# Scores of last queries and early blocks, made for an even and an odd head pair together

## The chip, the cores and the metric

The kernel runs on one core of a Trainium2 chip. The metric is the device time of one execution, in microseconds (us). The core has TensorE (PE in the profile; its weight loads are PEld), VectorE (DVE), ScalarE (ACT), GpSimd (POOL) and SyncE (SP, which issues the DMAs). SBUF is the working memory, PSUM the eight banks into which TensorE writes.

## What is computed

Attention of 4 batches x 8 heads over 576 positions with heads 64 wide, with a mask by blocks of 64 (a query sees its own block and all before it), then two MLPs over the 2304 tokens, 512 wide.

```python
scores = scale * np.matmul(q, k.transpose(0, 1, 3, 2))
mask = block_i >= block_j            # blocks of 64
scores = np.where(mask, scores, -1000000000.0)
attn = softmax(scores)               # exp(s - max) / (sum + 1e-09)
x = np.matmul(attn, v)               # -> (2304, 512)
x = (sigmoid(x @ w_gate) * (x @ w_val)) @ w_out      # d_ff 1536
h = x @ w_in                                          # d_ff 2048
return np.maximum(0.01 * h, h) @ w_out2
```

## The kernel before

**Stages.** Tokens are worked on in stages. Batch 0's attention runs alone at the front. Stage 0 is the MLP over tokens 0 to 767, with batch 1's attention beside it; stage 1 is the MLP over tokens 768 to 1279, with the attention of batches 2 and 3 beside it; a last stage does the other 1024 tokens with no attention (`pair_unit`, its products at L1149). The MLP's products beside attention are made in units of twelve matmuls at L1301, each into one of three PSUM banks (`b_mm`), which VectorE or ScalarE drains. Since 768 is not a multiple of 576, stage 0 also needs the first 192 queries of batch 1 and stage 1 the first 128 of batch 2 ahead of time: these are the early blocks (`first_blocks`, L688).

**Order.** Nothing is issued as it is written. Each step is an `op` with an engine, a cost, what it reads, writes and uses, and a due time; `Plan.order` (L149) simulates the five engines with these costs and fixes the order of instructions on each. A ring of buffers is handed out in the order in which the program asked for it. An engine then follows its order and waits on semaphores, so anything behind a waiting instruction on its engine waits too. A changed cost or dependency moves everything that the plan places after it.

**A head pair.** `attention` (L407) takes four pairs of heads (a = 0, 1) of a batch in turn. Queries and keys of a pair lie in one tile `tqk`, head 0 on partitions 0 to 63 and head 1 on 64 to 127; there are 3 such tiles, and 2 for V. `made_scores` (L599) makes the scores of query tiles 0 and 1, and of 2 and 3; `softmax` (L466) has VectorE mask, scale and find the least (L485), ScalarE take the exponential (L500), VectorE invert the sum (L510, L513) and ScalarE or GpSimd multiply (L518, L520); `transposed` (L622) turns the probabilities with TensorE (L633) into `tp` banks, of which there are two, and VectorE or ScalarE copies them to `p_t`; `p_v` (L648) is the product with V (L657). A batch whose first queries are made early starts with query tile 1.

**Last queries.** 576 is four tiles of 128 and a rest of 64. For the rest both heads share one tile of scores: `of_last` (L545) puts head a on output partitions 64a to 64a + 63, from input partitions 64a to 64a + 63, so that the two products use the upper left and the lower right quarter of TensorE's array (64 rows, 64 columns; the profile writes 64\*64). Beside the MLP the first 512 keys go to a `tp` bank and the last 64 to the free end of a score bank, at the line that also makes all other scores (L428); `alone`, they are two pieces of 288. `later` holds products that are issued with the next group of scores: the last queries' scores, then last P·V (L584, `last_p_v`) and P·V. The transposed probabilities (L569) of the last queries go to a tile of their own, `p_l` (named `last`), whose lower half is zero for the last 64 keys.

**Early blocks.** `first_blocks` makes the scores of all its pairs at L730, each pair's head 0 in the upper left and head 1 in the lower right quarter, in two groups of blocks by width, each with one score bank and one op. Batch 1 has two calls of two pairs (blocks of 64, 128 and 192 keys) at the end of batch 0's attention, batch 2 one call of four pairs (64 and 128 keys) ahead of batch 1's fourth pair (L1421). P·V of early blocks is at L773.

In the code a float32 product is one call; in the trace it stands as two matmul records of the same shape.

Of the kernel before, what the change touches and what calls it, by code (L numbers as in the profile page):

```python
# [18 lines left out]
P = 128  # L19
# [205 lines left out]
def block_attention_then_two_mlps(  # L225
# [51 lines left out]
    p_l = const.tile([P, NKT * P], F32, name="last")  # L277
# [23 lines left out]
    for c, n, turns_of in ((0, P, 2), (1, 2 * P, 2), (2, 3 * P, 1), (3, 4 * P, 1), (NKT - 1, S, 1)):  # L301
        for a in range(1 if n == S else 2):
            for k in range(turns_of):
                pp[c, a, k] = Lazy(lambda x=at_col, n=n: both[:, x:x + n])
                at_col += n
    assert at_col <= 16 * TN
    for k, x in (("first", (3, 0, 0)), ("second", (3, 1, 0))):
        pp[k] = pp[x]
    r_acc = ring("acc", 1, [P, 4 * SL])
# [97 lines left out]
    def attention(b, start, length, alone, others=()):  # L407
# [13 lines left out]
        def of_scores(products, toks, tqk):  # L421
# [3 lines left out]
            def f():  # L425
                for ps, col, row, a, q0, nq, k0, nk in products:
                    half = slice(a * D, a * D + D)
                    nc.tensor.matmul(  # L428
                        ps[row:row + nq, col:col + nk], lhsT=tqk[half, 0, q0:q0 + nq], rhs=tqk[half, 1, k0:k0 + nk],
                        start=True, stop=True,  # L430
                    )

            used = list(dict.fromkeys(x[0] for x in products))
            return sum(0.82e-3 * x[7] for x in products), f, [(tqk, 0), (tqk, 1)], toks, [tqk, *used]

        def scores(products, tqk, t, slack=slack):
            stretch([of_scores(products, list(dict.fromkeys(x[0] for x in products)), tqk)], t, slack)


        later = []  # L440
# [25 lines left out]
        def softmax(tiles, places, masked, t):  # L466
# [5 lines left out]
            for i, pieces in enumerate(tiles):  # L472
                x = places[i]
                p_tok, claim, keep = ("pp", *x), [], []
                if x[0] in pp:
                    w = pieces[0][2]
                    pt = Lazy(lambda x=x, w=w: pp[x[0]][:, x[1] - places[0][1]:x[1] - places[0][1] + w])
# [49 lines left out]
        def pair(i):  # L527
# [17 lines left out]
            def of_last(pieces):  # L545
# [9 lines left out]
            def last_queries(t):  # L555

                if alone:
                    pieces = [(p, 0, S // 2, p) for p in (bank(), bank())]
                    scores(of_last(pieces), tqk, t)
                else:  # L560
                    pieces = beside
                ((pt, p_tok),) = softmax([pieces], [(NKT - 1, 0, 0)], False, t)
                for part, (j0, j1) in enumerate(((0, NKT - 1), (NKT - 1, NKT))):
# [3 lines left out]
                    def f(tp=tp, nr=nr, j0=j0, j1=j1):  # L567
# [5 lines left out]
                    copy(  # L573
                        n, lambda nr=nr, j0=j0, n=n: p_l[:nr, j0 * P:j0 * P + n], lambda tp=tp, nr=nr, n=n: tp[:nr, :n],
                        [tp], [("last", part)], [tp], t + 4.4, True,
                    )

                def last_p_v(t):
                    px = (b_mm if alone else b_tp).tile()

                    def f():
                        for j in range(NKT):
                            for a in range(2):
                                nc.tensor.matmul(  # L584
                                    px[a * D:a * D + D, :BLK], lhsT=tv[:, a, j],
                                    rhs=p_l[:, j * P + a * BLK:j * P + (a + 1) * BLK], start=j == 0, stop=j == NKT - 1,
# [3 lines left out]
                        NKT * 0.116, f, [(tv, 0), (tv, 1), ("last", 0), ("last", 1)], [px], [px, tv],  # L590
                        lambda: split(S - BLK, S, "D", t + 0.8, px, [px]),
# [7 lines left out]
            def made_scores(cs, t):  # L599
# [905 lines left out]
```

## Time and profile before

| | |
|---|---|
| median of 3 runs | 985.93 us (985.16 to 987.45) |
| profiled execution | 985.49 us, its span 983.7 |
| granted TensorE clock | 1.0 of full speed |
| busy share of the span | PE 98%, DVE 79%, ACT 56%, POOL 17% |
| bytes moved | 227.52 MB, mean 231 GB/s |

The span runs from the first to the last instruction of the program; what lies around it belongs to the time too. PE's share counts the modelled ends of pipelined matmuls, so one that is always busy can still have started its matmuls later than possible: the start of the next operation is the safer measure of what a group takes. A wait is listed with what ended it. Rows of the timeline give the start, the length over all merged records, the engine, the line, the tile written and read, the array shape (rows\*columns), the tile of data, and how many records (x).

### The profile page before, as it was taken

What the parts mean: (1) busy time and instruction counts of PE and PEld (TensorE: products, weight loads), DVE (VectorE), ACT (ScalarE), POOL (GpSimd) and SP (SyncE); (2) the same over time, 40 slices, a digit from 0 to 9 for tenths busy, and PEclk for the clock granted to TensorE, in tenths of its full rate; (3) what the DMA queues carried; (4) which work ended last, traced back from release to release, by engine and by line L of the source; (5) the groups of instructions that cost most, each with busy time, mean ns of one, the idle gap of its engine ahead of it and who ended that gap; (6) DMA issues with size and microseconds to landing.
All of it is one profiled execution on the core that took longest, in us unless ns stands there. A gap on an engine that the chain in (4) does not pass through costs nothing.

```text
span 983.7 us, 15675 instructions
## 1 busy us (share of the span) xinstructions
PE 968.5 (98%) x5468; PEld 780.4 (79%) x5468; DVE 777.4 (79%) x1658; ACT 549.6 (56%) x1103; POOL 163.1 (17%) x172
## 2 busy tenths in 40 slices
PE   7999999999999999999999999999999999999998
PEld 4688888879888888778777877778888877888886
DVE  6989989889989847778789988985538479958656
ACT  7988776576766516455655575444526134744521
POOL 2422001221102101213432232120002021100000
PEclk9999999999999999999999999999999999999999
DMA  7488886856875636989888887877565555665664
GB/s 212 139 288 268 265 288 218 265 186 227 277 266 188 214 121 232 311 278 296 302 283 282 290 262 252 294 255 249 179 204 194 189 183 160 200 212 182 198 195 147
DMA packets 92718, 227.52 MB, mean 231 GB/s; under 512 B 9952, under 2 KB 29920, under 8 KB 92640
## 3 DMA queue, kind: packets, MB, share of 16 engines
q1 hardware_dynamic: 92640, 226.53, 69.6%
q8 instruction: 43, 0.70, 0.3%
q14 instruction: 35, 0.29, 0.1%
HBM read 150.47 MB, written 76.02 MB: 230 GB/s over the span
## 4 chain that ended last, share of the span: by engine, by line
PE 94%; DVE 2%; ACT 2%; DMA 1%; issue 0%; SPq 0%; ACTq 0%; DVEq 0%
PE mm L1301 47%; PE sc L1149 18%; PE tp L1149 9%; PE mm L1149 4%; PE tp L633 3%; PE sc L428 3%; PE pa L657 2%; PE tp L428 2%; PE tp L569 1%; DMA w<-ds 1%; PE mm L657 1%; PE tp L584 1%; ACT both L500 1%; ACT both L518 1%; DVE x L1221 0%; DMA qk<-in_qk 0%
## 5 line engine op out<-in xcount | busy, mean ns | idle before, releaser
L1301 PE MATMUL mm<-x,w 128*128 128x512 f32 (+2 forms) x1008 | 234.2, 384 | 0.0
L1301 PEld LDWEIGHTS mm<-x,w 128*128 128x128 f32 x1008 | 179.9, 188 | 38.5 <-issue 5.2
L1301 PE MATMUL mm<-g,w 128*128 128x512 f32 (+1 forms) x792 | 163.7, 358 | 0.0
L1301 PEld LDWEIGHTS mm<-g,w 128*128 128x128 f32 x792 | 130.2, 189 | 23.0 <-issue 2.4
L1149 PE MATMUL sc<-both,w 128*128 128x512 f32 x480 | 128.2, 390 | 0.1
L1149 PEld LDWEIGHTS sc<-both,w 128*128 128x128 f32 x480 | 89.9, 188 | 19.9 <-ACT wf L342 0.5
L500 ACT ACTIVATE both<-both,nm 128x256 f32<-128x256 f32 (+5 forms) x148 | 84.1, 570 | 28.3 <-DVE nm L485 27.6
L901 POOL TENSOR_TENSOR wf<-mag,rnd 128x512 int32<-128x512 int32 x28 | 37.3, 1332 | 205.9 <-DVE w L355 107.2
L887 ACT ACTIVATE mag<-raw 128x512 f32<-128x512 f32 x68 | 45.6, 671 | 42.8 <-POOL wf L901 18.1
L1301 PE MATMUL mm<-xa,w 128*128 128x256 f32 x480 | 63.6, 285 | 0.0
L1301 PEld LDWEIGHTS mm<-xa,w 128*128 128x128 f32 x480 | 60.8, 191 | 3.3 <-issue 0.8
L355 DVE TENSOR_TENSOR g<-gf,g 128x512 fp32r<-128x512 f32 (+2 forms) x73 | 56.8, 779 | 3.0 <-ACT g L342 3.0
L520 POOL TENSOR_SCALAR both<-both,r 128x256 f32<-128x256 f32 (+6 forms) x54 | 34.9, 653 | 114.3 <-DVE r L513 95.7
L342 ACT ACTIVATE g<-gf 128x512 fp32r<-128x512 f32 (+2 forms) x61 | 40.0, 657 | 24.1 <-DVE gf L1332 12.7
L518 ACT ACTIVATE both<-both,r 128x384 f32<-128x384 f32 (+6 forms) x94 | 48.7, 567 | 7.1 <-DVE r L513 7.0
L485 DVE CUSTOM_DVE_ANT_0 both<-sc,mask 128x256 f32<-128x256 f32 (+6 forms) x101 | 39.4, 423 | 16.1 <-PE sc L428 16.1
L1362 DVE TENSOR_TENSOR acc<-mm,acc 128x512 f32<-128x512 f32 (+1 forms) x60 | 35.8, 598 | 18.8 <-PE mm L1301 18.6
L1221 DVE TENSOR_TENSOR x<-sc,x 128x512 f32<-128x512 f32 x44 | 30.1, 689 | 22.3 <-PE sc L1149 22.2
L895 DVE SCALAR_TENSOR_TENSOR mag<-raw,mag 128x512 int32<-128x512 int32 x68 | 47.4, 698 | 0.3
L1301 PE MATMUL mm<-sg,w 128*128 128x512 f32 (+1 forms) x216 | 47.2, 354 | 0.0
L428 PE MATMUL sc<-qk 64*128 64x384 f32 (+5 forms) x228 | 41.9, 415 | 5.1 <-DMA qk<-in_qk 5.1
L355 DVE TENSOR_TENSOR w<-wf,w 128x512 fp32r<-128x512 f32 x68 | 46.5, 684 | 0.2
(255 smaller groups left out, 1843.7 us busy)
## 6 DMA issues: line engine op xcount, KB each, us to landing
w<-wd SPq DMA_DIRECT2D x102, 512.0 KB, 4.6
raw<-in_w SPq DMA_DIRECT2D x68, 512.0 KB, 4.4
wd<-w SPq DMA_DIRECT2D x68, 512.0 KB, 4.1
ds<-raw SPq DMA_DIRECT2D x68, 512.0 KB, 5.2
w<-ds SPq DMA_DIRECT2D x68, 512.0 KB, 4.3
qk<-in_qk SPq DMA_DIRECT2D x32, 288.0 KB, 5.7
w<-wd SPq DMA_DIRECT2D x68, 128.0 KB, 3.8
v<-in_v SPq DMA_DIRECT2D x32, 160.0 KB, 3.5
```

The costliest lines, as they stand in the source:

```text
L342: nc.scalar.activation(dst(), src(), AF.Copy)
L355: engines[e].tensor_tensor(dst(), a(), f32(b()), ALU.subtract)
L428: nc.tensor.matmul(ps[row:row + nq, col:col + nk], lhsT=tqk[half, 0, q0:q0 + nq], rhs=tqk[half, 1, k0:k0 + nk], start=True, stop=True,)
L485: nc.vector.tensor_tensor_reduce(out=pt[:, n:n + width], in0=ps[:, col:col + width], in1=mask[:, 4 * P + BLK - width:] if masked else mask ...
L500: nc.scalar.activation(pt[:, :n], pt[:, :n], AF.Exp, bias=nm[:, k - 1:k], scale=-1.0, accum_out=sm[:, i:i + 1],)
L518: nc.scalar.activation(pt[:, :n], pt[:, :n], AF.Copy, scale=r[:, i:i + 1])
L887: op("act", c_act(n), lambda: nc.scalar.activation(mag[:], words(1).bitcast(F32), AF.Abs), [raw], [mag], [raw, mag], d - 8)
L895: op("dve", c_dve(n), lambda: nc.vector.scalar_tensor_tensor(out=mag[:].bitcast(I32), in0=words(1).bitcast(I32), scalar=-0x40000000, in1=m ...
L901: engines[e].tensor_tensor(wf[:].bitcast(I32), mag[:].bitcast(I32), rnd[:], ALU.add)
L1149: nc.tensor.matmul(p[:, :n], lhsT=wt[:, wl, at * P:(at + 1) * P], rhs=view[:, xl], start=first and k == 0 and wl + xl == 0, stop=k == 1 an ...
L1301: nc.tensor.matmul(ps[:, :n], lhsT=ws[:, wl, k * P:(k + 1) * P], rhs=srcs[k]()[:, xl, hs], start=k == 0 and wl + xl == 0, stop=k == 3 and ...
L1362: op("dve", c_dve(n), lambda: nc.vector.tensor_tensor(a(), ps[:, :n], a(), ALU.add), [ps], toks_a, [ps, *host], e)
```

## The change

Beside the MLP, an even pair no longer makes the scores of its last queries. It leaves them to the odd pair that follows: `of_last` takes a `turn`, and in an odd pair (turn 1) head a's product goes to the other output half, so its two heads use the upper right and lower left quarter. The odd pair then issues one op with both pairs' products, alternating between the pairs, into two `tp` banks for the 512 keys and two score banks for the 64; its cost to the plan is halved. Softmax, transpositions and last P·V of the even pair are made right before those of the odd one; both last P·V come with the scores of the pair after that. `first_blocks` takes one score bank for its even and one for its odd pairs, turned in the same way, and makes all scores in one op; batch 2's call moves ahead of batch 1's third pair. The tile `p_l` goes: transposed probabilities of last queries lie in places of `p_t` that the causal order leaves free, one set for each turn, and two ops on GpSimd write the zeros. The probabilities of query tiles 0 and 1 have one set of places instead of two, those of last queries two instead of one. Nothing else is computed, and no product is dropped or added.

```diff
@@ -274,7 +274,6 @@
-    p_l = const.tile([P, NKT * P], F32, name="last")
@@ -298,14 +297,25 @@
-    for c, n, turns_of in ((0, P, 2), (1, 2 * P, 2), (2, 3 * P, 1), (3, 4 * P, 1), (NKT - 1, S, 1)):
-        for a in range(1 if n == S else 2):
-            for k in range(turns_of):
-                pp[c, a, k] = Lazy(lambda x=at_col, n=n: both[:, x:x + n])
-                at_col += n
+    for c, n in ((0, P), (1, 2 * P), (2, 3 * P), (3, 4 * P), (NKT - 1, S)):
+        for a in range(2):
+            pp[c, a] = Lazy(lambda x=at_col, n=n: both[:, x:x + n])
+            at_col += n
     assert at_col <= 16 * TN
-    for k, x in (("first", (3, 0, 0)), ("second", (3, 1, 0))):
+    for k, x in (("first", (3, 0)), ("second", (3, 1))):
         pp[k] = pp[x]
+
+    def p_last(turn, j):
+
+        if j < NKT - 1:
+            return p_t[:, 3 - turn, j // 2, j % 2 * P:(j % 2 + 1) * P]
+        return p_t[:, 1, 0, :P] if turn else p_t[:, 3, 0, 2 * P:3 * P]
+
+    for turn in range(2):
+        op(
+            "pool", 0.3, lambda turn=turn: nc.gpsimd.memset(p_last(turn, NKT - 1)[BLK:], 0.0), (), [("zeros", turn)], [both],
+            0.0,
+        )
...
@@ -418,26 +428,27 @@
-        def of_scores(products, toks, tqk):
+        def of_scores(products, toks, share=1.0):
...
-                for ps, col, row, a, q0, nq, k0, nk in products:
+                for tqk, ps, col, row, a, q0, nq, k0, nk in products:
...
-            used = list(dict.fromkeys(x[0] for x in products))
-            return sum(0.82e-3 * x[7] for x in products), f, [(tqk, 0), (tqk, 1)], toks, [tqk, *used]
-
-        def scores(products, tqk, t, slack=slack):
+            qks, used = [list(dict.fromkeys(x[k] for x in products)) for k in range(2)]
+            cost = share * sum(0.82e-3 * x[8] for x in products)
+            return cost, f, [(x, a) for x in qks for a in range(2)], toks, [*qks, *used]
+
+        def scores(products, t, slack=slack):
+            stretch([of_scores(products, list(dict.fromkeys(x[1] for x in products)))], t, slack)
+
+
+        later, waits = [], []
...
@@ -542,24 +553,24 @@
+            turn = 0 if alone else i % 2
+
+            def of_last(pieces, turn=turn, tqk=tqk):
                 n, r = 0, []
                 for p, col, width, _ in pieces:
-                    r += [(p, col, a * BLK, a, S - BLK, BLK, n, width) for a in range(2)]
+                    r.append([(tqk, p, col, (a ^ turn) * BLK, a, S - BLK, BLK, n, width) for a in range(2)])
                     n += width
                 return r
...
-            def last_queries(t):
+            def last_queries(t, lasts, pieces=None):
 
                 if alone:
                     pieces = [(p, 0, S // 2, p) for p in (bank(), bank())]
-                    scores(of_last(pieces), tqk, t)
-                else:
-                    pieces = beside
-                ((pt, p_tok),) = softmax([pieces], [(NKT - 1, 0, 0)], False, t)
+                    scores([y for x in of_last(pieces) for y in x], t)
+                ((pt, p_tok),) = softmax([pieces], [(NKT - 1, turn)], False, t)
...
-                    copy(
-                        n, lambda nr=nr, j0=j0, n=n: p_l[:nr, j0 * P:j0 * P + n], lambda tp=tp, nr=nr, n=n: tp[:nr, :n],
-                        [tp], [("last", part)], [tp], t + 4.4, True,
-                    )
+                    if part:
+                        to, of = (lambda: p_last(turn, NKT - 1)[:BLK]), (lambda tp=tp, n=n: tp[:BLK, :n])
+                    else:
+                        to = lambda: p_t[:, 3 - turn, :, :2 * P]
+                        of = lambda tp=tp, n=n: tp[:, :n].rearrange("p (a q) -> p a q", a=2)
+                    copy(n, to, of, [tp], [("last", turn, part)], [tp, both], t + 4.4, True)
...
+                                half = a ^ turn
                                 nc.tensor.matmul(
                                     px[a * D:a * D + D, :BLK], lhsT=tv[:, a, j],
-                                    rhs=p_l[:, j * P + a * BLK:j * P + (a + 1) * BLK], start=j == 0, stop=j == NKT - 1,
+                                    rhs=p_last(turn, j)[:, half * BLK:(half + 1) * BLK], start=j == 0, stop=j == NKT - 1,
...
-                        NKT * 0.116, f, [(tv, 0), (tv, 1), ("last", 0), ("last", 1)], [px], [px, tv],
-                        lambda: split(S - BLK, S, "D", t + 0.8, px, [px]),
+                        NKT * 0.116, f, [(tv, 0), (tv, 1), ("last", turn, 0), ("last", turn, 1), ("zeros", turn)], [px],
+                        [px, tv, both], lambda: split(S - BLK, S, "D", t + 0.8, px, [px]),
...
-                if cs[0] < 2 and not alone:
-                    p = b_tp.tile()
-                    beside.extend([(p, 0, 4 * P, p), (ps[cs[0], 0], 3 * P, BLK, (ps[cs[0], 0], "beside"))])
-                    later.insert(0, lambda t: of_scores(of_last(beside), [x[3] for x in beside], tqk))
+                if cs[0] < 2 and turn:
+                    for k in range(2):
+                        p = b_tp.tile()
+                        beside.append([(p, 0, 4 * P, p), (ps[cs[0], k], 3 * P, BLK, (ps[cs[0], k], "beside"))])
+                    products = [of_last(beside[0], *waits[0][1:]), of_last(beside[1])]
+                    later.insert(0, lambda t: of_scores(
+                        [z for x in zip(*products) for y in x for z in y], [x[3] for xs in beside for x in xs], 0.5
+                    ))
                 scores(
-                    [(ps[c, a], cols[c], 0, a, c * P, P, 0, (c + 1) * P) for c in cs for a in range(2)], tqk, t,
+                    [(tqk, ps[c, a], cols[c], 0, a, c * P, P, 0, (c + 1) * P) for c in cs for a in range(2)], t,
...
-                done = softmax([[made[x]] for x in xs], [(c, a, i % 2 if c < 2 else 0) for c, a in xs], True, t)
+                done = softmax([[made[x]] for x in xs], xs, True, t)
...
-                last_queries(at[NKT - 1])
...
-                last_queries(t)
+                if turn:
+                    waits.pop()[0](t, lasts, beside[0])
+                    last_queries(t, lasts, beside[1])
+                else:
+                    waits.append((last_queries, turn, tqk))
...
-            groups, at = [[]], 0
-            for k, width in enumerate(widths):
-                if at + m * width > 512:
-                    groups.append([])
-                    at = 0
-                groups[-1].append((k, at))
-                at += m * width
+            ps = [b_sc.tile(), b_sc.tile()]
+            tiles, at = [[], []], [0, 0]
+            for i in range(m):
+                for k, width in enumerate(widths):
+                    tiles[i % 2].append((k, i, at[i % 2], width))
+                    at[i % 2] += width
+
+            def f():
+                x = x_qk()
+                for xs in zip(*tiles):
+                    for p, (k, i, col, width) in zip(ps, xs):
+                        for a in range(2):
+                            half, row = slice(a * D, a * D + D), (a ^ i % 2) * BLK
+                            nc.tensor.matmul(
+                                p[row:row + BLK, col:col + width], lhsT=x[half, i, 0, k * BLK:(k + 1) * BLK],
+                                rhs=x[half, i, 1, :width], start=True, stop=True,
+                            )
+
+            stretch([(
+                sum(0.82e-3 * x[3] for xs in tiles for x in xs), f, [(tqk, i, a) for i in range(m) for a in range(2)], ps,
+                [tqk, *ps],
+            )], t)
...
-            for (place, tok), ks in zip((("first", ("pp", 3, 0, 0)), ("second", ("pp", 3, 1, 0))), groups):
...
-                def f(p=p, tiles=tiles):
-                    x = x_qk()
-                    for k, i, col, width in tiles:
-                        for a in range(2):
-                            half = slice(a * D, a * D + D)
-                            nc.tensor.matmul(
-                                p[half, col:col + width], lhsT=x[half, i, 0, k * BLK:(k + 1) * BLK], rhs=x[half, i, 1, :width],
-                                start=True, stop=True,
-                            )
-
-                stretch([(
-                    sum(0.82e-3 * 2 * x[3] for x in tiles), f, [(tqk, i, a) for i in range(m) for a in range(2)], [p], [tqk, p],
-                )], t)
-                done = softmax([[(p, col, width, p)] for _, _, col, width in tiles], [(place, x[2], tok) for x in tiles], False, t)
-                for x, y in zip(tiles, done):
+            for (place, tok), p, xs in zip((("first", ("pp", 3, 0)), ("second", ("pp", 3, 1))), ps, tiles):
+                done = softmax([[(p, col, width, p)] for _, _, col, width in xs], [(place, x[2], tok) for x in xs], False, t)
+                for x, y in zip(xs, done):
                     soft[x[0], x[1]] = *y, tok
...
+                                row = 3 * P + (a ^ i % 2) * BLK
-                                    rhs=p_t[:nr, jj, aa, 3 * P + a * BLK:3 * P + (a + 1) * BLK],
-                                    start=j == 0, stop=j == js[-1],
+                                    rhs=p_t[:nr, jj, aa, row:row + BLK], start=j == 0, stop=j == js[-1],
...
-                attention(1, starts[0] + 3, length - SPREAD, False, [(2, (0, 1, 2, 3), 3)])
+                attention(1, starts[0] + 3, length - SPREAD, False, [(2, (0, 1, 2, 3), 2)])
...
-        nc.gpsimd.memset(p_l[BLK:, (NKT - 1) * P:], 0.0)
```

## Rows read from the trace of the kernel before

**Rows 1.** The page, part 1: busy time, share of the span and instructions per engine.

```profile
PE 968.5 (98%) x5468; PEld 780.4 (79%) x5468; DVE 777.4 (79%) x1658; ACT 549.6 (56%) x1103; POOL 163.1 (17%) x172
```

**Rows 2.** Busy time by stretch: window, length, engines' busy us, granted clock, DMA share, GB/s.

```profile
300.00:340.00 40.00, 40.00 (x238) 34.31 (x237) 37.25 (x73) 25.15 (x48) 6.61 (x6) 1.00 0.60 204
```

**Rows 3.** The page, part 4: the chain that ended last, by engine.

```profile
PE 94%; DVE 2%; ACT 2%; DMA 1%; issue 0%; SPq 0%; ACTq 0%; DVEq 0%
```

**Rows 4.** PE's waits: what waited for what, us in total, times, longest.

```profile
PE sc L428 <- DMA qk<-in_qk: 5.1, 2, 4.8
PE tp L1149 <- DMA w<-ds: 2.1, 2, 1.6
PE tp L1149 <- DVE x L355: 0.9, 1, 0.9
...
PE sc L1149 <- DVE x L1221: 0.8, 1, 0.8
```

**Rows 5.** Timeline of PE, 206 to 209 us: the last queries of one pair.

```profile
206.94 1.08 PE L428 MATMUL tp<-qk 64*64 64x512 f32 x4
207.85 0.28 PE L428 MATMUL sc<-qk 64*64 64x64 f32 x4
208.06 0.80 PE L584 MATMUL tp<-last,v 128*64 128x64 f32 x20
```

**Rows 6.** The same timeline cut to 206.9 to 207.0 us.

```profile
206.94 0.65 PE L428 MATMUL tp<-qk 64*64 64x512 f32 x2
```

**Rows 7.** Timeline of PE, 70.72 to 70.78 us: early blocks' P·V, then last queries.

```profile
70.60 0.27 PE L773 MATMUL pa<-both,v 64*64 64x64 f32 x2
70.62 0.64 PE L428 MATMUL tp<-qk 64*64 64x512 f32 x1
70.70 0.22 PE L773 MATMUL pa<-both,v 64*64 64x64 f32 x2
```

**Rows 8.** Timeline of PE, 293.74 to 293.80 and 302.0 to 302.2 us.

```profile
293.75 0.27 PE L773 MATMUL tp<-both,v 64*64 64x64 f32 x2
...
302.09 0.60 PE L428 MATMUL tp<-qk 64*128 64x512 f32 x2
```

**Rows 9.** Timeline of PE, early blocks of batch 1 (45) and batch 2 (248).

```profile
45.58 1.54 PE L730 MATMUL sc<-qk 64*64 64x64 f32 x24
47.05 0.87 PE L657 MATMUL mm<-both,v 128*64 128x256 f32 x8
...
248.60 0.68 PE L730 MATMUL sc<-qk 64*64 64x64 f32 x16
249.21 0.80 PE L584 MATMUL tp<-last,v 128*64 128x64 f32 x20
...
251.89 1.09 PE L730 MATMUL sc<-qk 64*64 64x128 f32 x16
252.91 0.97 PE L1301 MATMUL mm<-x,w 128*128 128x512 f32 x3
```

**Rows 10.** Timeline of DVE, 438 to 440 us: a pair's last queries.

```profile
438.90 0.69 DVE L485 CUSTOM_DVE_ANT_0 both<-tp,mask 128x512 f32<-128x512 f32 x1
...
439.65 0.28 DVE L485 CUSTOM_DVE_ANT_0 both<-sc,mask,nm 128x64 f32<-128x64 f32 x1
```

**Rows 11.** The chain in order of time, 600 to 620 us: one MLP unit.

```profile
608.72 2.74 PE mm L1301 x12
```

**Rows 12.** Timeline of PE, 23.3 to 24.2 us, batch 0's attention.

```profile
23.34 0.87 PE L633 MATMUL tp<-ident,both 128*128 128x128 f32 x6
24.14 0.37 PE L428 MATMUL sc<-qk 64*128 64x128 f32 x1
```

**Rows 13.** Timeline of PE, 360 to 375 us: end of batch 1's attention.

```profile
360.11 0.80 PE L584 MATMUL tp<-last,v 128*64 128x64 f32 x20
...
368.81 1.59 PE L1301 MATMUL mm<-xa,w 128*128 128x256 f32 x12
```

**Rows 14.** The page, part 6: DMA issues of V, KB each, us to landing.

```profile
v<-in_v SPq DMA_DIRECT2D x32, 160.0 KB, 3.5
```

More of the change, by code (lines that the diff above doesn't have):

```diff
@@ L431, in f @@
                     )
-            used = list(dict.fromkeys(x[0] for x in products))
-            return sum(0.82e-3 * x[7] for x in products), f, [(tqk, 0), (tqk, 1)], toks, [tqk, *used]
-        def scores(products, tqk, t, slack=slack):
-            stretch([of_scores(products, list(dict.fromkeys(x[0] for x in products)), tqk)], t, slack)
-        later = []
+            qks, used = [list(dict.fromkeys(x[k] for x in products)) for k in range(2)]
[4 more added lines that the diff above has]
+        later, waits = [], []
         def stretch(parts, t, slack=slack):
@@ L476, in softmax @@
                     w = pieces[0][2]
-                    pt = Lazy(lambda x=x, w=w: pp[x[0]][:, x[1] - places[0][1]:x[1] - places[0][1] + w])
+                    pt = Lazy(lambda x=x, w=w: pp[x[0]][:, x[1]:x[1] + w])
                     claim, keep = ([], [x[2]]) if i else ([x[2]], [])
@@ L543, in split @@
                 keep(b, i, n0, n1, parts, t, p, base, reads)
-            def of_last(pieces):
+            turn = 0 if alone else i % 2
+            def of_last(pieces, turn=turn, tqk=tqk):
                 n, r = 0, []
                 for p, col, width, _ in pieces:
-                    r += [(p, col, a * BLK, a, S - BLK, BLK, n, width) for a in range(2)]
+                    r.append([(tqk, p, col, (a ^ turn) * BLK, a, S - BLK, BLK, n, width) for a in range(2)])
                     n += width
@@ L676, in pair @@
                     query_tiles(cs, made_scores(cs, at[cs[0]]), at[cs[0]])
-                last_queries(at[NKT - 1])
+                last_queries(at[NKT - 1], lasts)
             else:
@@ L712, in first_blocks @@
             widths = [(k + 1) * BLK for k in range(nb)]
-            groups, at = [[]], 0
-            for k, width in enumerate(widths):
-                if at + m * width > 512:
-                    groups.append([])
-                    at = 0
-                groups[-1].append((k, at))
-                at += m * width
-            soft = {}
-            for (place, tok), ks in zip((("first", ("pp", 3, 0, 0)), ("second", ("pp", 3, 1, 0))), groups):
-                p = b_sc.tile()
-                tiles = [(k, i, at + i * widths[k], widths[k]) for k, at in ks for i in range(m)]
-                def f(p=p, tiles=tiles):
-                    x = x_qk()
-                    for k, i, col, width in tiles:
-                        for a in range(2):
-                            half = slice(a * D, a * D + D)
-                            nc.tensor.matmul(
-                                p[half, col:col + width], lhsT=x[half, i, 0, k * BLK:(k + 1) * BLK], rhs=x[half, i, 1, :width],
-                                start=True, stop=True,
-                            )
-                stretch([(
-                    sum(0.82e-3 * 2 * x[3] for x in tiles), f, [(tqk, i, a) for i in range(m) for a in range(2)], [p], [tqk, p],
-                )], t)
-                done = softmax([[(p, col, width, p)] for _, _, col, width in tiles], [(place, x[2], tok) for x in tiles], False, t)
-                for x, y in zip(tiles, done):
```

## The prediction

> **What bounds the kernel now.** I read the page first: TensorE (PE) is busy for 98% of the span [rows 1], and in the stretch where VectorE is fullest its granted clock is 1.00, the 2.4 GHz level [rows 2]. The chain that ended last is PE for 94% [rows 3]. PE's list of waits shows what is left: 5.1 us for the first load at the start, and then single waits of up to 1.6 us, the largest in the last stage (L1149) [rows 4]. While attention runs beside the MLP PE has no gap to speak of: 40.00 busy in 40 us [rows 2]. So a microsecond of PE work taken out anywhere after the start should come off the end, as long as no other engine gets in its way; the sum is a sum of PE time. It is made against the profiled execution, 985.49 us (span 983.7 and 1.8 around it); the median of the runs is 985.93, 0.44 above.
>
> **Part 1, the last queries.** In one pair the scores of queries 512 to 575 are two pieces, 512 and 64 keys wide, for two heads. From the start of the first to the start of what follows they take 208.06 - 206.94 = 1.12 us: 0.91 for the 512 columns, 0.21 for the 64 [rows 5]. Each product stands as two records (four for two products [rows 5]), so 0.91 is two steps of some 0.43 us and a switch of 0.05. Both heads already share these steps: two records stand within 0.65 us [rows 6], where one alone spans 0.64 [rows 7]. They sit on the diagonal quarters of the array (head 0 on rows and columns 0 to 63, head 1 on 64 to 127). The change keeps an even pair's pieces back, turns the odd pair's heads onto the other two quarters and issues all four products together. There are 12 such pairs beside the MLP (the alone attention of batch 0 keeps its old form), so six groups of 1.12 us vanish: 6.72 us, if four run as two do. What the two further starts add to each of the six groups no row shows; between nothing and 0.2 us (one more 64-column piece, 0.21 [rows 5]), I take 0.05, since starts inside a step lie hundredths apart [rows 6]. Part 1: 6.72 - 0.30 = **6.4 us**, bounds 5.5 and 6.7.
>
> Do four run as two do? The trace has no four, but it has each ingredient. Two products that share array rows and differ in columns overlap (two of 0.27 us within 0.27), and two that share columns and differ in rows do too (two of 0.60 within 0.60) [rows 8]. And by chance it has three: at 70.60 two products of an early block, on the left and right half of rows 0 to 63, are followed at 70.62 by a last-queries record, which starts before the second records of those two, at 70.70 [rows 7]. With rows 0 to 63 taken, only head 1's quarter was free for it, though head 0's product stands ahead of it in the code. So a record on a free quarter passes several that wait. I weigh this against a rule of the Trainium skill ("TensorE: Matmul & The Clock Gate", Part 3, "What overlaps and what doesn't"), which has matmuls start and end in strict program order. By it head 1 could not start before head 0's second record, and a pair's 512 columns would take three steps, 1.29 us; the sum would have a loss in place of part 1. The trace does not agree: they take 0.91 [rows 5].
>
> **Part 2, the early blocks.** Batch 1's two calls, alone at the front, each take 47.05 - 45.58 = 1.47 us [rows 9]; batch 2's call takes 0.61 and 1.02 us in two bursts [rows 9]. Now the even and odd pairs share steps, so the streamed columns halve. A call of batch 1 drops 2 x (64 + 128 + 192) = 768 columns; at 0.43 us for 512 that is 0.64 us, twice 1.28. Batch 2's drops 4 x (64 + 128) = 768 too, and one of two entries of some 0.15 us: 0.8. Part 2: **2.1 us**, bounds 1.6 (batch 2's columns and three quarters of batch 1's, since PE has small gaps at the front) and 2.3 (half of all four bursts).
>
> **What is moved.** The softmax work of an even pair's last queries now comes with the odd pair's: VectorE (DVE) gets in one go 0.69 + 0.28 us of scores [rows 10] and the small reads, sum and reciprocal behind them, some 1.5 us (an estimate), ScalarE as much. Behind it on DVE stand the drains of MLP results. DVE is busy for 37.25 of 40 us in its fullest stretch with an odd pair [rows 2], so the lump may lag for ten microseconds or more; but three PSUM banks serve the MLP, and a unit fills one in 2.74 us [rows 11], so PE stops only when DVE is over 5 us late. I cost it at nothing; without that cover it is 6 x 1.5 = 9 us. The joint product takes both transposition banks, and the odd pair's third and fourth query tiles wait for DVE to clear them, about 1.1 us later than now; PE has MLP units to run meanwhile. The single set of probability tiles for query tiles 0 and 1 (there were two) adds a wait of DVE for the previous pair's transpositions. Beside the MLP pairs lie tens of microseconds apart; alone, those transpositions already run just before the scores that need the place, at 23.34 and 24.14 [rows 12]: nothing, or at most 0.3 us for each of three pairs.
>
> An even pair's last P·V is made after the odd one's scores, so the last pairs of a batch end with two such products instead of one. After batch 1 it stands at 360.11, and units in stage 0's form run until 370.4 [rows 13], so 0.8 us of PE [rows 5] and some 1 us of copies more are covered. V is held longer for the same reason: the loads of V for batch 2's early blocks, moved from before the fourth pair to before the third, must now wait on SyncE's queue until the first two pairs' last P·V is done, with weight loads behind them. A load of V lands in 3.5 us [rows 14], against tens of microseconds until a pair's V is used; I cost it at nothing, at most 1 us. The zeros in the new places, written by GpSimd at the start, lie under PE's wait for the first load [rows 4].
>
> **The sum.** 985.49 - 6.4 - 2.1 = 977.0 for a profiled execution; 0.44 on top for the median gives **977.4 us**. What can't be worked out is the plan: the order on every engine is computed from costs, so each edit moves the instructions after it. The waits that the order decides are 3.8 us in [rows 4] (without the first load); they can double, or go but for a quarter. With the bounds of both parts, 985.93 - 9.0 - 2.9 = 974.0 to 985.93 - 7.1 + 3.8 = 982.6.
>
> **The rivals.** *The plan gives back half.* Weight loads, the drains or the last stage take up what PE saves: PE arrives earlier at places where a load already lands last (1.6 us at the worst [rows 4]). For it: DVE at 93% [rows 2]. Against: PE had no gap there. Four more waits like that worst one would cost 4 to 6 us: 980 to 984, about 982.
>
> *Only pairs overlap.* The two new quarters wait for the old ones; then the change does not do what it says. The columns take as long as before and only six switches of 0.1 to 0.2 us go: 985.93 - 1 = 985. For it: no row has four products at once. Against: [rows 7].
>
> *The four quarters take turns, and it is slower.* If a product whose array rows or columns are shared with a neighbour waits for that neighbour's both records, the joint group loses even the overlap of today: 8 steps of 0.43 and 8 of 0.05 are 3.8 us against 2 x 1.12 = 2.24, six times 1.6, and the early blocks double to 3 x 1.3 more: 985.93 + 9.6 + 3.9 = 999. If a product waits only until the one issued before it is in its second record, a group takes five steps where two pairs now take four: six times some 0.45 us more and about 1 us for the early blocks, 989 or a little over. That is what the skill's rule of program order would make of it. The rival decides at one place: a second or third product of a group that starts a whole step (0.43 us) after the first instead of hundredths. [Rows 7 and 8] speak against it.
>
> **How the numbers follow.** Forecast 0.75 (974 to 981), giving back 0.13 (980 to 984), only pairs 0.06, slower 0.06 (turns, or the lump on DVE with its cover gone). The likeliest gives 977.4. The range 974.0 to 982.6 leaves out the last two, the worst end of the second and a little below: about 2 in 10. A measurement here tells about 0.2%, 2.0 us, from no change: faster means below 983.96. Forecast and nearly all of giving back lie there: 0.86 faster, 0.08 same, 0.06 slower.
>
> **What would show it.** In the profile after: six groups of last-queries records at L428 beside the MLP instead of twelve, each with eight records of 512 columns, from the first of which to the next operation pass about 1.17 us, not 2.2; early-block bursts of 0.8 us; PE's busy time down by 8 to 9 us, its list of waits no longer than now; DVE's and ScalarE's busy time unchanged. I am wrong in the parts if a group takes over 1.5 us, in the cover if a wait of PE for DVE stands behind an odd pair, and in the plan if L1149's waits grow.

## The result, and the profile after

The changed kernel takes **977.43 us** (median of 4 runs, 976.75 to 979.91) against 986.69 for the kernel before on the same chip: ratio 0.9908 [0.988, 0.9936]. Two repeats beside the experiments, after_again and after_third, gave 977.53 (0.9912 [0.9896, 0.9927]) and 978.90 (0.9922 [0.9908, 0.9935]). The 977.53 is the median of after_again's three fast runs, 977.13 to 979.43: a fourth run took 2457.44 us, slow throughout and for a reason that stays open, and with it the median would be 978.48. Ratios are taken over the runs and need not be exactly the quotients of the medians. Forecast: 977.4.

The changed kernel's lines are numbered otherwise: scores L428 is now L438, early blocks' scores L730 is L748 and their P·V L773 is L795, last P·V L584 is L598, P·V L657 is L675, transpositions L633 is L651, DVE's masking L485 is L496, MLP units L1301 is L1322, `pair_unit` L1149 is L1170.

First the timeline of PE around one group of last queries (start, length over the merged records, engine, line, tiles, array shape, data, records), and the same cut to its first 0.07 us; it answers to [rows 5, 6].

```profile
250.03 1.09 PE L438 MATMUL tp<-qk 64*64 64x512 f32 x8
250.94 0.29 PE L438 MATMUL sc<-qk 64*64 64x64 f32 x8
251.16 2.16 PE L675 MATMUL pa<-both,v 128*64 128x384 f32 x16
...
250.03 0.66 PE L438 MATMUL tp<-qk 64*64 64x512 f32 x4
```

Eight records of 512 columns where there were four, in the same 0.91 us, and the whole group takes 251.16 - 250.03 = 1.13 us, against 1.12 for half the work in [rows 5]. Four records stand within 0.66 us, where one alone spans 0.64 [rows 7]: four products share each step. There are six such groups, each of 1.13.

The early blocks, answering to [rows 9] (PE's timeline, batch 1's two calls and batch 2's one):

```profile
46.59 0.95 PE L748 MATMUL sc<-qk 64*64 64x64 f32 x24
47.67 0.87 PE L675 MATMUL mm<-both,v 128*64 128x256 f32 x8
...
53.51 0.89 PE L748 MATMUL sc<-qk 64*64 64x64 f32 x24
54.33 0.80 PE L598 MATMUL mm<-both,v 128*64 128x64 f32 x20
...
203.78 0.90 PE L748 MATMUL sc<-qk 64*64 64x64 f32 x32
```

Batch 1's calls go from 1.47 to 1.08 and 0.82 us; the first ends in a small gap (0.95 of 1.08 busy). Batch 2's two bursts of 0.61 and 1.02 became one of 0.83, to the next start at 204.61.

The page's busy times (part 1) and PE's waits (total, times, longest), which answer to [rows 1, 4]:

```profile
PE 962.0 (98%) x5468; PEld 775.7 (79%) x5468; DVE 777.3 (79%) x1662; ACT 546.2 (56%) x1101; POOL 169.2 (17%) x171
...
PE sc L438 <- DMA qk<-in_qk: 5.0, 2, 4.6
PE tp L1170 <- DMA w<-ds: 2.4, 2, 1.3
PE tp L651 <- DVE both L354: 1.0, 2, 0.7
PE tp L1170 <- DVE x L365: 0.9, 1, 0.9
PE sc L1170 <- DVE x L1242: 0.8, 1, 0.8
PE sc L438 <- DVE nm L496: 0.5, 1, 0.5
...
PE tp L651 <- ACT both L352: 0.3, 1, 0.3
```

The longest wait of attention in the list of the kernel before:

```profile
PE tp L633 <- ACT both L342: 0.8, 1, 0.8
```

PE's busy time fell by 6.5 us. Two waits for DVE are new: 1.0 us of transpositions, and 0.5 us of scores (L438 behind L496). In return transpositions wait 0.3 us for ScalarE, where it was 0.8. Without the first load the whole list came to 6.1 us before and comes to 6.6. The profiled execution took 979.91 us, the slowest of the four, with a span of 977.8 against 983.7 before. A part of that was not the change. The same eight records at the front, first before, then after:

```profile
11.07 1.22 PE L428 MATMUL sc<-qk 64*64 64x288 f32 x8
...
11.40 2.18 PE L438 MATMUL sc<-qk 64*64 64x288 f32 x8
```

The clock record of the trace has the full level granted from 10.52 us before and from 14.07 after; over all eleven profiles of the changed kernel and of the variants below that have such a record that point lies anywhere from 10.4 to 14.9 us. Here it cost about 0.94 us (start-to-start time of all scores of the front, 20.45 before and 21.39 after).

Where the time went, added up from starts: the first product of the last stage stood at 638.36 before and stands at 632.14, 6.22 earlier.

```profile
638.36 1.52 PE L1149 MATMUL sc<-both,w 128*128 128x512 f32 x6
...
632.14 1.52 PE L1170 MATMUL sc<-both,w 128*128 128x512 f32 x6
```

The groups give 12 x 1.12 - 6 x 1.13 = 6.66 and the early blocks (1.47 - 1.08) + (1.47 - 0.82) + (0.61 + 1.02 - 0.83) = 1.84, together 8.50. Take off 0.94 for the front and 0.2, by which the waits ahead of the last stage grew in sum (2.3 to 2.5, without the first load): 7.4, and 6.22 are seen. Most of the difference is in the products of the MLP units beside attention (L1301, now L1322): the same records take 0.97 us more from start to start, 470.24 against 469.27, with no wait among them. In diagonal below they take 0.86 more, so this comes with the new order and not with the quarters. A third of it is seen: scores follow a 512-column unit product at 14 places instead of 10, and such a product takes 0.32 us to the next start, against 0.23 where another unit product follows. For the rest no cause is shown. From there to the end of the span the changed kernel takes 0.3 us more (345.7 against 345.3).

### The profile page after: what moved, and what is told of

It reads as the page before. It is cut to its first block, busy times and chain, and to the rows that moved or that the text cites. A ratio compares the mean times of both kernels' runs of the same rounds, so it can differ in the third digit from the quotient of the medians.

```text
span 977.8 us, 15698 instructions
## 1 busy us (share of the span) xinstructions
PE 962.0 (98%) x5468; PEld 775.7 (79%) x5468; DVE 777.3 (79%) x1662; ACT 546.2 (56%) x1101; POOL 169.2 (17%) x171
## 4 chain that ended last, share of the span: by engine, by line
PE 92%; DVE 3%; DMA 3%; ACT 1%; issue 0%; SPq 0%; DVEq 0%
PE mm L1322 46%; PE sc L1170 18%; PE tp L1170 9%; PE mm L1170 4%; PE sc L438 3%; PE tp L651 3%; PE pa L675 2%; PE tp L438 2%; DMA w<-ds 1%; PE mm L675 1%; PE tp L580 1%; PE tp L598 1%; PE pa L438 1%; DMA w<-wd 1%; DMA ds<-raw 1%; ACT both L511 1%
## 5 line engine op out<-in xcount | busy, mean ns | idle before, releaser
L1322 PE MATMUL mm<-x,w 128*128 128x512 f32 (+2 forms) x1008 | 235.1, 385 | 0.0
L1322 PEld LDWEIGHTS mm<-x,w 128*128 128x128 f32 x1008 | 179.8, 188 | 39.5 <-issue 6.1
L1322 PE MATMUL mm<-g,w 128*128 128x512 f32 (+1 forms) x792 | 163.6, 358 | 0.0
L1322 PEld LDWEIGHTS mm<-g,w 128*128 128x128 f32 x792 | 130.1, 189 | 22.7 <-issue 2.8
L1170 PE MATMUL sc<-both,w 128*128 128x512 f32 x480 | 128.3, 390 | 0.1
L1170 PEld LDWEIGHTS sc<-both,w 128*128 128x128 f32 x480 | 89.9, 188 | 19.9 <-ACT wf L352 0.5
L1322 PE MATMUL mm<-xa,w 128*128 128x256 f32 x480 | 63.8, 285 | 0.0
L1322 PEld LDWEIGHTS mm<-xa,w 128*128 128x128 f32 x480 | 60.9, 191 | 3.5 <-ACT mag L908 0.8
L531 POOL TENSOR_SCALAR both<-both,r 128x384 f32<-128x384 f32 (+6 forms) x53 | 36.3, 691 | 137.7 <-DVE r L524 113.5
L352 ACT ACTIVATE g<-gf 128x512 fp32r<-128x512 f32 (+2 forms) x53 | 35.0, 662 | 31.7 <-DVE gf L1353 18.6
L529 ACT ACTIVATE both<-both,r 128x512 f32<-128x512 f32 (+6 forms) x95 | 49.3, 571 | 5.3 <-DVE r L524 4.8
L365 DVE TENSOR_TENSOR w<-wf,w 128x512 fp32r<-128x512 f32 x68 | 49.2, 727 | 1.1 <-ACT w L352 0.9
L962 POOL TENSOR_TENSOR wf<-w 128x512 f32<-128x512 f32 x26 | 36.2, 1397 | 77.6 <-DMA w<-wd 34.8
L496 DVE CUSTOM_DVE_ANT_0 both<-sc,mask 128x256 f32<-128x256 f32 (+6 forms) x101 | 39.1, 422 | 11.7 <-PE sc L438 11.5
L365 DVE TENSOR_TENSOR raw<-raw 128x1024 fp32r<-128x1024 f32 x34 | 42.6, 1252 | 6.8 <-DMA ds<-raw 6.0
```

Of the source, the lines that this page charges most:

```text
L365: engines[e].tensor_tensor(dst(), a(), f32(b()), ALU.subtract)
L496: nc.vector.tensor_tensor_reduce(out=pt[:, n:n + width], in0=ps[:, col:col + width], in1=mask[:, 4 * P + BLK - width:] if masked else mask ...
L529: nc.scalar.activation(pt[:, :n], pt[:, :n], AF.Copy, scale=r[:, i:i + 1])
L531: nc.gpsimd.tensor_scalar(out=pt[:, :n], in0=pt[:, :n], scalar1=r[:, i:i + 1], scalar2=0.0, op0=ALU.mult, op1=ALU.add)
L962: lambda e: engines[e].tensor_tensor(out(), x(), y(), alu), reads, writes, uses, d, port=True,
L1170: nc.tensor.matmul(p[:, :n], lhsT=wt[:, wl, at * P:(at + 1) * P], rhs=view[:, xl], start=first and k == 0 and wl + xl == 0, stop=k == 1 an ...
```

## Experiments

Each compares with the kernel before on its own chip (medians 986.6 to 987.2). after_again, diagonal, last_only and early_only ran together, then pair_after_pair, full_cost, lump_x2 and lump_x4, then after_third and grouped, then grouped2.

**Is it the quarters?** In diagonal every product goes back to the diagonal quarters; the instructions and their order on every engine stay those of the changed kernel.

```diff
-  r.append([(tqk, p, col, (a ^ turn) * BLK, a, S - BLK, BLK, n, width) for a in range(2)])
+  r.append([(tqk, p, col, a * BLK, a, S - BLK, BLK, n, width) for a in range(2)])
-  half, row = slice(a * D, a * D + D), (a ^ i % 2) * BLK
+  half, row = slice(a * D, a * D + D), a * BLK
```

> The changed kernel with every product back on the diagonal quarters; all that was moved, joined or delayed stays, and the order of instructions on each engine is the changed kernel's. Theory A (the gain is that four quarters run at once): six groups of last queries take about 2.15 us instead of 1.13 and the three early bursts some 0.64 us more each, so 6 x 1.0 + 3 x 0.64 = 8 us slower than the changed kernel, about 985.5, no more than a microsecond from the kernel before. Theory B (the gain comes from the new order and fewer switches, not from the array): no slower than the changed kernel, 977 to 978.5. If moving and joining cost something of their own, it shows as more than the time before: 987 or over.

Measured: 985.11 us, 0.9981 [0.9972, 0.999], where the changed kernel beside it (after_again) took 977.53.

> The changed kernel once more, as the measure for the runs beside it. If the gain is PE work taken out, as forecast: 977.4 us, within 1.5, and 8 to 9.5 us under the kernel before.

PE's timeline of diagonal, one group, whole and cut to its first 0.1 us:

```profile
253.10 1.93 PE L438 MATMUL tp<-qk 64*64 64x512 f32 x8
254.87 0.40 PE L438 MATMUL sc<-qk 64*64 64x64 f32 x8
255.20 2.16 PE L675 MATMUL pa<-both,v 128*64 128x384 f32 x16
...
253.10 0.65 PE L438 MATMUL tp<-qk 64*64 64x512 f32 x2
```

The group is 2.10 us long and starts with two records at a time, not four. Six times 2.10 - 1.13, and 1.7 more in the early blocks (bursts of 1.47, 1.47 and 1.49 us against 1.08, 0.82 and 0.83), make 7.5 us by rows; the medians differ by 7.6. So 7.6 of the 9.6 us that after_again gains are the two further quarters. Joining and moving as such cost nothing in sum; diagonal is even 2.0 us faster than before, where no more than one was expected. Of these the groups' saved switches are 12 x 1.12 - 6 x 2.10 = 0.84; the rest is not placed.

**Which part gives what?** last_only takes the early blocks back to the old form, early_only the last queries. early_only is the kernel before with the change's hunk of `first_blocks` alone, last_only the changed kernel without it; the middle of that hunk:

```diff
-  half = slice(a * D, a * D + D)
+  half, row = slice(a * D, a * D + D), (a ^ i % 2) * BLK
-  p[half, col:col + width], lhsT=x[half, i, 0, k * BLK:(k + 1) * BLK], ...
+  p[row:row + BLK, col:col + width], lhsT=x[half, i, 0, k * BLK:(k + 1) * BLK], ...
```

> The change to the last queries alone; the early blocks are made as in the kernel before (batch 2's still ahead of the third pair). Theory A: 1.9 to 2.1 us slower than the changed kernel, 979.5. Theory B, with the order deciding: anything within 3 us of it, on either side.

> The change to the early blocks alone, the last queries as before. Theory A: the two bursts at the front shorter by 0.64 us each and batch 2's by 0.8, so 2.1 us under the kernel before, 984. If what PE gains at the front is lost again in waits there: 985 or more.

Measured: last_only 980.63 us, 0.994 [0.9927, 0.9952], a median 6.5 us under the kernel before; early_only 983.78, 0.9967 [0.9958, 0.9977], 3.4 us under it. In early_only's trace the bursts sum to 2.74 us (start to start) where they were 4.57, a gain of 1.83, as in the changed kernel; the other 1.5 us of its median are not placed. last_only stands 3.1 us over after_again, where 1.9 to 2.1 were expected. The plan orders each of the two anew, which was not tried apart. Within that the parts add up (9.9 against 9.6 for the whole beside them).

**Does the order of issue matter?** pair_after_pair issues all products of the even pair, then all of the odd pair, where the change alternates.

```diff
-  [z for x in zip(*products) for y in x for z in y], [x[3] for xs in beside for x in xs], 0.5
+  [z for x in products for y in x for z in y], [x[3] for xs in beside for x in xs], 0.5
```

> In each group of last queries the even pair's four products (512, then 64 keys) are issued before the odd pair's, instead of alternating; all else as in the changed kernel. If a record on a free quarter passes every record that waits on another, the odd pair's first records still start hundredths of a microsecond after the even pair's: a group takes 1.13 to 1.25 us and the time is that of the changed kernel, 977.5. If it passes only a few, the odd pair starts after the even pair's first or second step: a group takes 1.6 to 2.1 us and the time is 980.5 to 983.5.

Measured: 978.15 us, 0.9916 [0.9903, 0.9928]. Its PE timeline, a group, and the cut to its first 0.08 us:

```profile
250.12 1.10 PE L438 MATMUL tp<-qk 64*64 64x512 f32 x8
251.03 0.31 PE L438 MATMUL sc<-qk 64*64 64x64 f32 x8
251.26 2.16 PE L675 MATMUL pa<-both,v 128*64 128x384 f32 x16
...
250.12 0.67 PE L438 MATMUL tp<-qk 64*64 64x512 f32 x4
```

Four records run at once here too, though the second passes of the even pair's products stand ahead of the odd pair's first ones in the code; those even passes start only at 250.60, after all four first ones. Alternating is worth 0.01 us a group (1.14 against 1.13).

**What is the plan's share?** full_cost keeps every operation and tells the plan the whole cost of the joint products, of last queries and of early blocks, so that it orders the rest anew. Its expectation speaks of the same instructions in another order; the plan also chooses anew which engine does copies and multiplications that two engines share (ScalarE has 1094 instructions instead of 1101, GpSimd 178 instead of 171).

```diff
-  [z for x in zip(*products) for y in x for z in y], [x[3] for xs in beside for x in xs], 0.5
+  [z for x in zip(*products) for y in x for z in y], [x[3] for xs in beside for x in xs], 1.0
...
-  sum(0.82e-3 * x[3] for xs in tiles for x in xs), f, ...
+  sum(0.82e-3 * 2 * x[3] for xs in tiles for x in xs), f, ...
```

> The changed kernel, with the plan told the full cost of the joint products (as if four ran as two after two) instead of half; the same instructions in another order. It measures what the order alone is worth. If the gain is PE work taken out and the order matters little: 977.5 within 1.5. If the order decides: more than 2 us off, on either side.

Measured: 981.10 us, 0.995 [0.9937, 0.9962]: 2.95 us over pair_after_pair on the same chip, from the plan's order and choice of engines alone, and more than the 2 us that were set as the mark. PE's waits in it that differ most:

```profile
PE tp L651 <- ACT both L352: 1.6, 2, 0.9
PE tp L651 <- DVE both L354: 1.4, 2, 0.9
```

They are 3.0 us, against 1.3 in the changed kernel (the 1.0 above and 0.3 for ACT), so some 1.7 are seen. The profiled execution, 979.99 us, is the fastest of full_cost's five and only 1.1 us above pair_after_pair's, so its trace can't place the whole 2.95.

**How much cover has the lump on DVE?** lump_x2 and lump_x4 make DVE's passes over the last queries' scores, beside the MLP, two and four times, with the same result.

```diff
+  for _ in range(2 if not masked and places[0][0] == NKT - 1 and not alone else 1):
       nc.vector.tensor_tensor_reduce(
```

> The changed kernel with VectorE making each pass over the last queries' scores twice beside the MLP (with the same result): 0.69 + 0.28 + 0.17 = 1.1 us more VectorE work for a pair, 2.3 us in one lump at an odd pair, 13.7 us in all; the order on every other engine is unchanged. If the lump on VectorE is covered by the three PSUM banks: 977.5 to 978.5. If it reaches PE: 980 to 991.

> The same with four passes instead of one: 3.4 us more for a pair, 6.8 us at an odd pair on top of what is there, 41 us in all. By the cover of some 5 us PE should now wait behind odd pairs, 2 to 4 us each: 985 to 1000. If the time stays under 979, the cover is larger than forecast.

Measured: lump_x2 981.55 us, 0.9954 [0.9938, 0.9969]; lump_x4 1017.36, 1.0309 [1.0295, 1.0324], well over the 985 to 1000 that were expected. The passes were cheaper than expected: DVE's busy time rose by 8.9 and 32.1 us instead of 13.7 and 41. PE's waits for the masking, lump_x2 first:

```profile
PE sc L438 <- DVE nm L496: 2.3, 1, 2.3
```

```profile
PE sc L438 <- DVE nm L496: 14.8, 5, 5.9
```

The place is behind the odd pairs. In the changed kernel, PE's and DVE's timelines there:

```profile
525.60 2.37 PE L675 MATMUL pa<-both,v 128*64 128x512 f32 x16
528.47 1.08 PE L438 MATMUL sc<-qk 64*128 64x384 f32 x4 [0.50 <-DVE nm L496]
529.19 1.22 PE L438 MATMUL tp<-qk 64*128 64x512 f32 x4
530.35 3.94 PE L1322 MATMUL mm<-x,w 128*128 128x512 f32 x16
...
525.70 0.29 DVE L496 CUSTOM_DVE_ANT_0 both<-sc,mask 128x128 f32<-128x128 f32 x1
...
526.82 0.69 DVE L496 CUSTOM_DVE_ANT_0 both<-tp,mask 128x512 f32<-128x512 f32 x1
...
527.42 0.69 DVE L496 CUSTOM_DVE_ANT_0 both<-tp,mask 128x512 f32<-128x512 f32 x1
...
528.24 0.28 DVE L496 CUSTOM_DVE_ANT_0 both<-sc,mask,nm 128x64 f32<-128x64 f32 x1
```

DVE reads through from 525.70 until its next operation starts at 528.45, and only then is the score bank free for the odd pair's third and fourth query tiles (L438 at 528.47). The MLP unit that could fill the time stands behind them, at 530.35. The even pair's two pieces take 0.60 and 0.21 of these steps: without them DVE would be done at 527.64, before P·V ends at 527.97, so by this sum the wait is the lump's. It is one place of six; at the other five PE had other products in between and the list shows no wait. In lump_x2 the same lines read:

```profile
524.98 2.38 PE L675 MATMUL pa<-both,v 128*64 128x512 f32 x16
529.66 2.15 PE L438 MATMUL sc<-qk 64*128 64x384 f32 x4 [2.30 <-DVE nm L496]
531.07 2.29 PE L438 MATMUL tp<-qk 64*128 64x512 f32 x4
533.29 0.97 PE L1322 MATMUL mm<-x,w 128*128 128x512 f32 x3
...
529.70:533.10 3.40, 3.40 (x8) 1.81 (x8) 3.18 (x16) 3.40 (x8) 2.40 (x3) 0.50 0.21 53
```

The last row is the stretch's busy times and, third from its end, the granted clock: 0.50, the 1.2 GHz level, right after PE had stood still for 2.30 us. The eight records took 533.29 - 529.66 = 3.63 us instead of 530.35 - 528.47 = 1.88. So 1.80 us of longer wait and 1.75 of lower clock: 3.55 in the profiled execution (981.66 us), and the medians differ by 3.4 (981.55 - 978.15, pair_after_pair being the measure of the changed kernel on this chip). The fall is not there in every run: of lump_x2's six, three have a mean granted clock of 0.998 (981.45 to 985.70 us), as the profiled one, and three of 1.0 (980.26 to 982.23). In lump_x4 the waits grow by 14.3, and a mean granted clock of 0.986 over 1012.9 us means 28 us at the lower level, worth at most 14 of lost work; other waits of PE that are new in its list add about 5. That is 33 of the 36.8 us by which the profiled execution, 1014.99, stands over pair_after_pair's median; the rest is not placed.

**A faster version.** In the early blocks' P·V products with 64 keys (64 array rows) and 128 keys alternate. grouped issues those with 128 rows first. It parts the two products that add up batch 1's third blocks, and so does not sum these whole; it stands for its time alone. grouped2 keeps the two side by side; its edit:

```diff
-  for i in range(m):
-      for k in range(nb):
+  order = [(i, k, j) for k in ((1, 0) if nb == 2 else (1,)) for i in range(m) for j in range((k + 2) // 2)]
+  if nb > 2:
+      order += [(0, 2, 0), (0, 2, 1), *((i, 0, 0) for i in range(m)), (1, 2, 1), (1, 2, 0)]
```

> The changed kernel as it is, once more, beside grouped. All theories: 977 to 979 us.

> The changed kernel with one more edit: in the early blocks' P.V of batches 1 and 2 the products with 128 keys are issued first and those with 64 keys last, where now the two kinds alternate. Same instructions, same data, same order on every engine otherwise. Theory (a change of the number of array rows that a product occupies costs about 0.1 us each, whoever shares the array): the 64-product bursts of P.V get shorter, by some 2 us in all, and the time is 975 to 976.5. Rival (the steps between these products are set by loading the 64-column weights, in whatever order): the bursts keep their length and the time is the changed kernel's, 977 to 979.

> As grouped, but batch 1's third blocks keep their two products (128 and 64 keys) side by side, since both add into one place of PSUM: 128-key products first, then one block's 128 and 64, the first blocks' 64, and the other third block's 64 and 128. The number of array rows changes twice within a burst of batch 1 and once within batch 2's, where in the changed kernel it changes at nearly every product. Theory of the switch: bursts of 1.4 to 1.5 us in batch 1 (1.74 in the changed kernel, 1.30 in grouped), 1.3 in batch 2, and a time of 975.5 to 977, about 2 us below the changed kernel's. Rival: back to 978 to 979.

Measured: after_third 978.90 us, 0.9922 [0.9908, 0.9935]; grouped 976.50, 0.9899 [0.9886, 0.9913]; grouped2 976.74, 0.9901 [0.9884, 0.9918]. Batch 2's burst and what follows, after_third first, then grouped2:

```profile
219.05 2.18 PE L795 MATMUL tp<-both,v 64*64 64x64 f32 x32
221.16 4.44 PE L1322 MATMUL mm<-g,w 128*128 128x256 f32 x24
```

```profile
219.15 1.30 PE L796 MATMUL tp<-both,v 128*64 128x64 f32 x32
220.38 4.44 PE L1325 MATMUL mm<-g,w 128*128 128x256 f32 x24
```

The same 32 records take 2.11 and 1.23 us. The number of rows changes seven times in the first and once in the second: 0.88 / 6 = 0.147 us a change. Batch 1's bursts agree: 1.67 us with four changes, 1.38 in grouped2 with two (0.145 each), 1.23 in grouped with one (0.147 each). By rows grouped2 saves 0.88 + 2 x 0.29 = 1.46 us; the median fell by 2.2, with intervals that still overlap. Its median is the lowest of the versions that compute the whole; that it is faster is shown by the rows, and by the times alone not yet.

## Why the prediction was right, and where it was not

**Part 1** held: groups of 1.13 us where 1.17 was forecast, 6.66 us against 6.4, inside its bounds. That four products run as two do rested on a chance meeting of three records [rows 7], and it carried over. The Trainium skill's rule ("TensorE: Matmul & The Clock Gate", Part 3, "What overlaps and what doesn't") that matmuls start in strict program order was set aside in the prediction; pair_after_pair bears that out: records of the odd pair's 512 keys run from the first 0.04 us of a group, and the even pair's products with 64 keys, issued ahead of them, start 0.91 us into it.

**Part 2** gave 1.84 against 2.1. The term that was too large is the first call, 0.39 instead of 0.64: there, PE ends the burst with a gap, as its lower bound allowed for.

**What is moved** was costed at nothing. For V's loads that held: no wait of PE for V is in the list, and a load lands in 3.9 us where it took 3.5 [rows 14]. For the DVE lump the cost was nearly right (0.5 us) and the reason wrong. The step that failed is "PE stops only when DVE is over 5 us late", with MLP units to run meanwhile. PE takes its instructions in the planned order, and what stands next behind an odd pair is its own third and fourth query tiles, which need the bank that DVE is still reading. The cover at the tightest of the six places was already used up: 0.5 us of wait after the change, 2.3 with the passes doubled. A wait of PE for DVE behind an odd pair was the sign I had named for a wrong cover, and it is there.

**The plan**: a term of its size was needed, since full_cost moves the time by 2.95 us with no product changed. The 3.8 us in the sum were misread, though: they are the three waits of the last stage that [rows 4] shows, and the whole list without the first load comes to 6.1. In the changed kernel transpositions wait 0.5 us more in sum and L1170 0.3, and the MLP units' 0.97 us, for which the prediction had no term, come with the new order. Whether the transpositions' waits come from the lump or from the order was not tried apart.

**The signs**: six groups of eight records, yes. PE busy down by 8 to 9: 6.5, or 8.5 (to 960.0) in after_third, where the front's clock rose as early as before. DVE unchanged (777.4 to 777.3), ACT 3 us less. PE's list of waits grew by 0.5 us without the first load, where it was to be no longer; the lump's 0.5 is one of several changes in it.

**The rivals**: *only pairs overlap* was priced at 985, and diagonal, which does just that, took 985.11. That close a hit is luck: the price was 1 us under a kernel before of 985.93, and diagonal is 2.0 under one of 987.16. *Quarters take turns* fell with the first group. *The plan gives back half* did not happen, but full_cost shows how near it lay: 981.1.

**The number**: 977.43 where 977.4 was forecast is closer than the working deserves. The two parts came to 8.50 us, as forecast, but by rows some 2.1 of them were lost again, to the clock at the front, the waits and the units, in an execution 2.5 us slower than the median. The forecast was a gain of 8.5 us from 985.93; the three measured gains are 9.3, 9.6 and 7.9 us, from medians of 986.7 to 987.2.

## What to carry to other kernels

When small products leave quarters of the array empty, look for a partner whose outputs can be turned onto them, and count in the trace of before how many records already stand in flight at once; their order in the code hardly mattered in the one other order that was tried. When work is lumped to make that possible, look for cover in what stands next on the waiting engine in its actual order, not in the work that the engine has in general. Where products of different row counts follow each other, sort them.

## What I had not expected of the hardware

- A change of the number of array rows between neighbouring products costs 0.145 to 0.147 us, three times over (batch 2, batch 1 in grouped and grouped2), where it was no term of mine at all.
- A stop of PE of 2.30 us was followed by 3.4 us at half the clock (lump_x2), which nearly doubled its price; the 0.50 us stop of the changed kernel was followed by none. Length alone does not decide it: in lump_x4 a wait of 2.94 us that ended at 487.48 was followed by a granted clock of 1.00 up to 492, and half of lump_x2's runs show none in their mean clock.
- The point at which the full clock is first granted moved between 10.4 and 14.9 us from profile to profile; in the changed kernel's own it cost 0.94 us, about a seventh of part 1's gain.
